# A bucketed attention and a mixture of eight experts in one kernel: where the subtractions of the weights' low halves, the places' matmul, the collection and the remaining capacity stand in the order of work

## The chip, the cores and the metric

The kernel runs on one core of one Trainium2 chip. The metric is device time of one launch in microseconds (us). Engines are named as in the profile: TensorE (PE, its weight loads PEld), VectorE (DVE), ScalarE (ACT), GpSimd (POOL) and SyncE (SP).

## The reference

Attention of 4 x 8 heads over 768 positions of width 64, where a query sees only keys of its own bucket (six signs of a projection), gives x of 3072 tokens by 512. Then a mixture of eight experts, in which the pairs of token and expert are taken in falling order of their score until every expert has its 384 tokens:

```python
cap = N // E                               # 3072 // 8 = 384
logits = x @ w_gate
for idx in np.argsort(-logits.flatten()):
    tok, e = (int(idx) // E, int(idx) % E)
    if assigned[tok] >= 0 or counts[e] >= cap: continue
    assigned[tok] = e
    counts[e] += 1
for e in range(E):
    mask = assigned == e
    h = np.maximum(x[mask] @ w1[e], 0.0)   # 512 x 1024
    out[mask] = h @ w2[e]                  # 1024 x 512
```

## The kernel before

The first 442 us are the attention and the scores; the change leaves them alone. The rest goes expert by expert, in the order in which experts fill up. `run()` (L816 to L852) writes this part out as **slots**, 68 for each expert: 32 slots of `layer1` (three matmuls L775 each) and 36 of `layer2` (two matmuls L787 each). The arithmetic is done in halves: a number is a 16-bit high half and a 16-bit low half, and a product is three matmuls, high by high, low by high and high by low.

**The weights' low halves.** `wload` (L716, GpSimd's indirect DMA) fetches the f32 weights of an expert, `wsplit` cuts them in quarters: ScalarE writes the high half `wh` and scales `wf` (L725, L726), and two subtractions of 128x512 for each quarter make `wl` = `wf` - `wh`. They are put in the list `s.pend`, each with the slot at which it is due. Three places take them from it: `hand(n)` gives n of them to GpSimd (L737), after a small copy `ztick` (L736) that makes GpSimd wait for the step of the moment; `fill()` gives one to VectorE (L741); and a due one is forced on GpSimd by `run()` (L847).

**Choosing the next expert's tokens.** Beside the matmuls of expert k runs phase p = k+1, a generator `phase()` whose parts are put at slots by the tables `EV` (phases 2 to 7; `EV[p]` for p under 5, else `EV[0]`) and `E1` (phase 1). A pair (c0, R) in `EV` gives the first slot, relative to the expert's first, and the distance R of the levels. The parts of a phase, in order:

- the first counting (`count` L504, L505 on TensorE; its last matmul L505 reads `nrem`, the remaining capacity, which ScalarE writes at L567), then the digits (L488) and the comparison L587 on VectorE, at c0;
- the hit (matmul L593, then L597 and a comparison L493 on VectorE), at c0+3;
- four levels of counting (`count4`, at c0+6, c0+6+R, ...) and hit (three slots later), and a last counting at c0+6+4R that ends in `satl` (L604);
- the step that closes the threshold at c0+9+4R (matmuls L607, L608, then on VectorE L611 to L619 with the members' mask `STb`, the weight index `zwidx` L700 and a running sum `cum` L632);
- the **places** (matmuls L635, L636 of `STb` and `cum`), at c0+13+4R, after which VectorE makes the one-hot `ohp` (L644) and `Rr` (L669);
- the **collection** (24 matmuls L646), at c0+22+4R, then the index L688, `close()` (L661 to L667: the new capacity `rem`, the mask `un`), the gather of the tokens (L708) and the next phase's scores and first wide comparison (L475 to L493).

At each part `hand` is called with the number from the list `HS` (phase 1: `H1`). `fill()` is called after the hit of the first counting (L593), after L608, after the places and after the collection. `XD` shifts the slots of the transposes `xsplit` of phases 1 to 3.

Of the kernel before, what the change touches and what calls it, by code (L numbers as in the profile page):

```python
# [14 lines left out]
ALU = mybir.AluOpType  # L15
# [5 lines left out]
 E0=[3, 5],  # L21
 E1=[3, 4],
 X=[2, 2, 5],
# [14 lines left out]
 OPS='b0 i3 i2 t0 b1 w5 r0 r2 w4 s0 w4 C1 r1 t1 c1 s1 B0 c0 D0 w2 w1 s4 w5 s2 s3 r3 v2 w5 v0 l0 l1 C0 m0 s5 w3 s6 r5 w2 l3 e0 e1 d0 u0 u1 s7 v1 l2 w0 m1 e2 | s8 | x0 | w0 | x1 s9 | r4 s10 | | | s11 m2 v3 f0 | x3 | | x2 | m3 | | | | | |')  # L38
PAT,E0,E1,DW,LEAD=(AP[k] for k in ('PAT','E0','E1','DW','LEAD'))
NB=dict(S=2,T=3,V=1)  # L40
# [337 lines left out]
SH=[25,20,15,10,5,0]  # L378
LOW=[1,1,1,1,1,0]
NT=[128,32,32,32,32,32]  # L380
E1=[-12,-4,-3,2,6,8,10,13,16,19,22,25,28,31,34,37,40,48]
H1=[0,0,0,0,0,2,0,2,0,2,0,2,0,2,1,0,0,0]
EV=[(-18,8),(0,0),(-6,7),(-10,7),(-14,7)]
WL=[4,46]
W1=[44,51,58,63]
WS=[0,57,52,48]
HS=[0,1,0,2,0,2,0,3,0,3,1,0,0,0]
BY=[-1,8,40]
W2=[2,7,12,17]
XS=[56,56,57,57]  # L390
XD=[0,7,4,0]
KW=[1,0,4,0,2,19,7,1]
SC=16
XSC=8.0
# [1 line left out]
class Moe:  # L396
# [142 lines left out]
    def phase(s,ph):  # L539

        nc,NC=s.nc,s.NC; V=nc.vector; T=nc.tensor; G_=nc.gpsimd
# [3 lines left out]
        def ps(): return s.ps0() if first and s.ps0 else s.ps()  # L545
# [3 lines left out]
        if not last:  # L549
            P=s.Z  # L550
            D,E,mxu=P["D"],P["E"],P["mxu"]; d=E[:,0]
            CMP=[P["cmp"][l and 1+l%2] for l in range(6)]
            if not first:
                for i,f in enumerate(s.best(P,0,NC)):
                    if ph==1 and i==4: yield
                    f()
                s.gate=P["OH"][0:1,0,0:1]
                for c0,c1_ in ((0,12),(12,NC)) if ph==1 else ((0,NC),):
                    if ph==1: yield
                    s.compare(CMP[0],0,d,c0,c1_)  # L560
                if ph==1: s.gate=CMP[0][0:1,NC//2-1,0,0:1]
            tot=0
            for l,w in enumerate(WID):
                tot+=w; u=2.0**-tot; cmp=CMP[l]
                yield
                pc=ps()
                if l==0 and not first: nc.scalar.mul(s.nrem,s.rem,-1.0/128)  # L567
                if l==0 or first:
                    for c0,c1_ in blocks if first else ((0,NC),):
                        if l: s.compare(cmp,l,d,c0,c1_)  # L570
                        s.count(pc,P,cmp,l,c0,c1_)
                    if first:
                        if l==0: wp=s.wps(); s.warm(KW[7],wp)
                        s.warm(KW[0],wp)
                    for a,b in ((l+1,l+2),) if first else ((1,6),):
                        if a<6:
                            for q in range(a,b): s.digit(P,q,slice(0,NC))
                            if first: V.tensor_tensor(E[:,a:b],D[:,a:b],s.sc[:,a:b],op=ALU.mult)
                            else:
                                for q in range(a,b): nc.scalar.activation(E[:,q],D[:,q],AF.Copy,scale=2.0**-sum(WID[:q+1]))  # L580
                else:
                    nt=s.count4(pc,P,cmp)

                if l==5: break
                sat=t([128,8],BF,"sat"); hit=t([128,1],BF,"hit"); J=NT[l]
                if l==0 or first:
                    V.tensor_scalar(sat[0:J],pc[0:J,0:8],0.0,0.0,op0=ALU.is_ge,op1=ALU.max,accum_out=hit[0:J])  # L587
                else:
                    V.tensor_tensor(sat[0:32],pc[96:128,24:32],nt,op=ALU.is_ge)
                    V.reduce_max(hit[0:32],sat[0:32],axis=AX.X)  # L590
                if not first: yield
                pn=ps(); n=pn[:,0:1]
                T.matmul(n,s.us[l][0:J],hit[0:J],start=True,stop=True)  # L593
                if first: s.warm(KW[1],wp)
                elif l==0: s.fill()
                d2=t([128,NC],BF,"d2",bufs=6); s.gate=d2[0:1,0:1]
                V.scalar_tensor_tensor(d2,d,n,E[:,l+1],op0=ALU.subtract,op1=ALU.add)  # L597
                if not first:
                    s.compare(CMP[l+1],l+1,d2); s.gate=CMP[l+1][0:1,NC//2-1,0,0:1]
                d=d2  # L600

            sat=t([128,8],BF,"satl"); s.gate=sat[0:1,0:1]; nn=t([128,1],F32,"nn"); nf=t([128,1],F32,"nf")
            if first: V.tensor_scalar(sat[0:32],pc[0:32,0:8],0.0,None,op0=ALU.is_ge)
            else: V.tensor_tensor(sat[0:32],pc[96:128,24:32],nt,op=ALU.is_ge)  # L604
            if not first: yield
            pe=ps()
            T.matmul(pe[:,0:8],s.ones,s.wtb,start=True,stop=False)  # L607
            T.matmul(pe[:,0:8],s.tiny[0:32],sat[0:32],start=False,stop=True)  # L608
            if first: s.warm(KW[2],wp)
            else: s.fill()  # L610
            V.reduce_max(nn,pe[:,0:8],axis=AX.X)  # L611
            wg=t([128,NC],F32,"wg"); e0=t([128,NC],F32,"e0"); A1=t([128,8,NC],BF,"A1"); cc=t([128,8],BF,"cc")
            V.tensor_scalar(nf,nn,ROUND*2.0**-32,ROUND*2.0**-32,op0=ALU.add,op1=ALU.subtract)
            V.scalar_tensor_tensor(wg,d,nn,mxu,op0=ALU.is_gt,op1=ALU.mult)
            V.tensor_scalar(cm,nn,nf,2.0**32,op0=ALU.subtract,op1=ALU.mult)
            V.tensor_tensor(s.asg,s.asg,wg,op=ALU.add)
            V.scalar_tensor_tensor(e0,d,nf,mxu,op0=ALU.is_equal,op1=ALU.mult)
            V.tensor_scalar(STb[:,0:NC],s.asg,cm,None,op0=ALU.is_equal)
            V.tensor_scalar(STb[:,NC:],e0,cm,None,op0=ALU.is_equal)  # L619
            s.widx(ph,cm,t)  # L620
        else:
            s8=t([128,8],F32,"s8"); e0=t([128,NC],F32,"e0")
            V.tensor_scalar(c1,s.rem,4.0e4,None,op0=ALU.is_lt)
            V.tensor_tensor(s8,c1,s.wt,op=ALU.mult)
            V.reduce_max(cm,s8,axis=AX.X)
            s.widx(ph,cm,t)
            V.tensor_scalar(e0,s.asg,cm,None,op0=ALU.is_equal)
            V.tensor_tensor(STb[:,0:NC],e0,s.un,op=ALU.add)
            V.memset(STb[:,NC:],0.0)
# [29 lines left out]
        def close(pq):  # L659

            bnd=t([128,8],F32,"bnd")  # L661
            V.tensor_tensor(s.rem,s.rem,pq,op=ALU.subtract)
            V.tensor_scalar(bnd,s.wt,cm,-3.0e38,op0=ALU.is_equal,op1=ALU.mult)
            V.scalar_tensor_tensor(s.rem,bnd,-5.0e4/3.0e38,s.rem,op0=ALU.mult,op1=ALU.add)
            V.tensor_tensor(s.Lm,s.Lm,be(bnd),op=ALU.add)
            V.scalar_tensor_tensor(s.un,wg,0.0,s.un,op0=ALU.is_equal,op1=ALU.mult)
            V.tensor_tensor(s.un,s.un,acc,op=ALU.subtract)  # L667
        def rr():
            for i in range(2): V.tensor_tensor(Rr[:,i],Gt[:,None,i:i+3].to_broadcast([128,2,3,NC]),s.gp[:,i,:,None,:].to_broadcast([128,2,3,NC]),op=ALU.mult)  # L669
        if first:  # L670
            pi=ps()
            for i,b in enumerate(blocks):
                members(*b)
                if not i: rr()
                collect(*b); s.warm(KW[4],wp)
        else:
            members(0,NC)
            rr()
            if not last: left()
            yield  # L680
            pi=ps()
            collect(0,NC)
            if not last:
                T.matmul(pp[:,64:72],s.ones,cc,start=True,stop=True)
                s.fill()
        idx=t([128,3],I32,"idx",bufs=4)
        with nc.allow_low_precision("whole numbers"):
            V.reduce_sum(idx,pi[:,0:12].rearrange("p (z c) -> p c z",z=4),axis=AX.X)  # L688
# [127 lines left out]
    def run(s):  # L816
        V=s.nc.vector; ch=s.ch; at={}; NS=68
# [6 lines left out]
        for p in range(1,8):  # L824
            b=NS*(p-1)
            c0,R=EV[p] if p<5 else EV[0]
            c=[c0,c0+3]
            for l in range(4): c+=[c0+6+R*l,c0+9+R*l]
            c+=[c0+6+4*R,c0+9+4*R,c0+13+4*R,c0+22+4*R]
            ev=[b+e for e in (E1 if p==1 else c)]  # L830
            hs=H1 if p==1 else HS
            dec=ev[-3]
            if p==7: ev=ev[-2:]; hs=[0,0]
            for e,n in zip(ev,hs): add(e,step,p,n)
            add(ev[-1],end,p)
            add(max(dec,b+WL[0]),s.wload,p,0); add(max(ev[-1],b+WL[1]),s.wload,p,1)
            for q in range(4):
                add(b+(WS[p]+4*q if p<4 else W1[q]),s.wsplit,p,0,q,None,b+NS+BY[0]+BY[1]*q if p<6 else 0)
                add(b+XS[q]+(XD[p] if p<4 else 0),s.xsplit,p,q)
        for k in range(8):  # L840
# [64 lines left out]
```

## Time and profile before

| | |
|---|---|
| median of three runs | 771.43 us (770.33 to 774.11) |
| the profiled execution | 773.31 us; its span 771.5 us |
| busy in the span: TensorE, its weight loads | 691.7 us (90%), 441.9 us (57%) |
| VectorE, ScalarE, GpSimd | 546.3 us (71%), 466.6 us (60%), 500.0 us (65%) |
| instructions | 19049 |

All times of single instructions are of the profiled execution, counted from the start of its span. In a timeline an instruction's row ends with the idle time of its engine before it and what ended that; where rows of the same kind follow one another, one row with xcount stands for them. "Granted clock" is the share of TensorE's 2.4 GHz that the chip granted, so 0.5 is 1.2 GHz.

### The profile page before, as it was taken

What the parts mean: (1) busy time and instruction counts of PE and PEld (TensorE: products, weight loads), DVE (VectorE), ACT (ScalarE), POOL (GpSimd) and SP (SyncE); (2) the same over time, 40 slices, a digit from 0 to 9 for tenths busy, and PEclk for the clock granted to TensorE, in tenths of its full rate; (3) what the DMA queues carried; (4) which work ended last, traced back from release to release, by engine and by line L of the source; (5) the groups of instructions that cost most, each with busy time, mean ns of one, the idle gap of its engine ahead of it and who ended that gap; (6) DMA issues with size and microseconds to landing.
All of it is one profiled execution on the core that took longest, in us unless ns stands there. A gap on an engine that the chain in (4) does not pass through costs nothing. (4 is left out here: it accounts for less than half of the span.)

```text
span 771.5 us, 19049 instructions
## 1 busy us (share of the span) xinstructions
PE 691.7 (90%) x7789; PEld 441.9 (57%) x7789; DVE 546.3 (71%) x1170; ACT 466.6 (60%) x858; POOL 500.0 (65%) x445
## 2 busy tenths in 40 slices
PE   8898898999999999988896688888898999999995
PEld 2566665767667667666675544444444555555452
DVE  4979978889888798987756667495868777743120
ACT  6677675677776777755561272817465565656550
POOL 8586859696886969755571546364648384858571
PEclk9999999999999999999997599999999999999998
DMA  7637655428254372500000525334160717162610
GB/s 185 172 102 208 156 148 126 117 73 202 91 127 117 107 196 65 132 29 23 22 22 23 174 86 168 120 120 167 43 258 28 259 42 260 42 221 86 250 45 41
DMA packets 39951, 93.57 MB, mean 121 GB/s; under 512 B 4548, under 2 KB 30520, under 8 KB 37816
## 3 DMA queue, kind: packets, MB, share of 16 engines
q1 hardware_dynamic: 33048, 46.21, 22.8%
q0 software_dynamic: 6816, 46.15, 16.9%
q8 instruction: 61, 1.00, 0.5%
q14 instruction: 26, 0.21, 0.1%
HBM read 59.53 MB, written 12.58 MB: 93 GB/s over the span
## 5 line engine op out<-in xcount | busy, mean ns | idle before, releaser
L255 POOL TENSOR_TENSOR lo<-pt 128x768 f16<-128x768 f32 x143 | 233.4, 1645 | 80.4 <-ACT pt L252 71.0
L252 ACT ACTIVATE pt<-pst 128x384 f32<-128x384 f32 x384 | 182.7, 491 | 95.5 <-PE pst L251 83.5
L228 DVE TENSOR_REDUCE m<-pss 128x1 f16<-128x770 f32 x192 | 182.3, 955 | 41.2 <-PE pss L226 40.1
L250 PE MATMUL pst<-qa,ka 128*128 128x384 f16 x384 | 125.1, 326 | 5.8 <-DVE XT L294 3.1
L251 PE MATMUL pst<-qb,kb 128*128 128x384 f16 x384 | 125.0, 326 | 0.0
L267 PE MATMUL psv<-vh,lo 128*128 128x65 f16 x1152 | 121.1, 194 | 3.3 <-POOL lo L255 3.3
L266 PE MATMUL psv<-vl,pt 128*128 128x64 f16 x1152 | 121.3, 193 | 0.0
L265 PE MATMUL psv<-vh,pt 128*128 128x65 f16 x1152 | 121.2, 195 | 0.0
L265 PEld LDWEIGHTS <-pt 128*128 128x128 bf16 x1152 | 106.7, 98 | 12.7 <-issue 3.1
L266 PEld LDWEIGHTS <-pt 128*128 128x128 bf16 x1152 | 105.8, 99 | 9.6
L226 PE MATMUL pss<-ka,qa 128*128 128x385 f16 x384 | 94.9, 329 | 14.6 <-DVE m L228 13.2
L267 PEld LDWEIGHTS <-lo 128*128 128x128 f16 x1152 | 105.8, 97 | 3.8 <-POOL lo L255 3.7
L725 ACT ACTIVATE wh<-wf 128x1024 f16<-128x1024 f32 x64 | 67.1, 1049 | 33.9 <-PE psa L693 21.1
L737 POOL TENSOR_TENSOR wl<-wf,wh 128x512 f16<-128x512 f32 x71 | 81.2, 1159 | 0.0
L775 PEld LDWEIGHTS <-wh 128*128 128x128 f16 x512 | 48.4, 100 | 33.3 <-issue 5.3
L726 ACT ACTIVATE wf<-wf 128x1024 f32<-128x1024 f32 x62 | 65.5, 1057 | 2.0
L778 DVE SCALAR_TENSOR_TENSOR hl<-px,hh 128x384 f16<-128x384 f32 x64 | 34.7, 552 | 43.7 <-ACT hh L777 43.4
L226 PEld LDWEIGHTS <-qa 128*128 128x128 f16 x384 | 37.4, 98 | 46.2 <-issue 23.7
L787 PEld LDWEIGHTS <-hh 128*128 128x128 f16 x384 | 36.8, 100 | 45.2 <-issue 9.2
L255 DVE TENSOR_TENSOR lo<-pt 128x768 f16<-128x768 f32 x49 | 61.7, 1258 | 1.5 <-ACT pt L252 1.0
L777 ACT ACTIVATE hh<-px 128x384 f16<-128x384 f32 x64 | 30.4, 481 | 49.7 <-PE px L775 49.7
L775 PE MATMUL px<-xl,wh 128*128 128x384 f16 x256 | 57.5, 337 | 0.0
(251 smaller groups left out, 1319.7 us busy)
## 6 DMA issues: line engine op xcount, KB each, us to landing
vp<-in_vv_dram SPq DMA_DIRECT2D x8, 768.0 KB
x_dram<-X SPq DMA_DIRECT2D x16, 384.0 KB
qp<-in_qT_dram SPq DMA_DIRECT2D x7, 768.0 KB
kp<-in_kT_dram SPq DMA_DIRECT2D x7, 768.0 KB
qa<-qh SPq DMA_DIRECT2D x14, 192.0 KB
ka<-kh SPq DMA_DIRECT2D x14, 192.0 KB
qb<-qh SPq DMA_DIRECT2D x14, 192.0 KB
kb<-kh SPq DMA_DIRECT2D x14, 192.0 KB
```

What stands on the lines that cost most here:

```text
L226: T.matmul(ps[:,hf,0:HK],QA[u][:,j,qc*128:qc*128+128],KA[u][:,j,hf*HK:hf*HK+HK],start=True,stop=True)
L228: V.tensor_reduce(M6[h][:,qc:qc+1],ps[:,:,0:HK],axis=AX.XY,op=ALU.max,negate=True)
L250: T.matmul(ps[:,0:384],KA[u][:,j,kr],QA[u][:,j,r],start=True,stop=False)
L251: T.matmul(ps[:,0:384],KB[u][:,j,kr],QB[u][:,j,r],start=False,stop=True)
L252: A.activation(PT[h,kc][0][:,r],ps[:,0:384],AF.Exp,scale=0.125)
L255: eng.tensor_tensor(l,p,p.bitcast(BF)[:,1::2],op=ALU.subtract)
L265: T.matmul(av[:,c,:],ph[:,r],VH[u][:,j,kc,:],start=(kc==0 and c==0),stop=False,skip_group_check=True)
L266: T.matmul(av[:,c,0:64],ph[:,r],VL[u][:,j,kc,:],start=False,stop=False,skip_group_check=True)
L267: T.matmul(av[:,c,:],l[:,r],VH[u][:,j,kc,:],start=False,stop=False,skip_group_check=True)
L725: s.nc.scalar.mul(h[:,r],f[:,r],WSC)
L737: for _ in range(n): s.nc.gpsimd.tensor_tensor(*s.pend.pop(0)[1],op=ALU.subtract)
L775: T.matmul(p[:,0:384],a[:,o:o+128],b[:,d],start=n==0,stop=n==11)
```

## The change

It moves the parts of a phase and the subtractions between them:

- `EV` and `E1`: the first slot is one later for phases 2 and 5 to 7 (p = 2: -6 to -5; p of 5 and more: -18 to -17) and two later for phases 3 and 4; phase 1 keeps its slots up to the places. The places are six slots behind the step before them in place of four (`c0+15+4R`), in phase 1 five in place of three; the collection is eight slots behind the places in place of nine, in phase 1 seven in place of eight.
- `HS` and `H1`: the number of subtractions given to GpSimd at each part; none at the first two parts and none after the last counting, three at three of the levels.
- `fill()`: not any more after L608; a new one after the digits of the first counting, ahead of L587; a second one after the collection.
- `nrem` is written by VectorE at the end of `close()` (L667 of the changed kernel) in place of by ScalarE at the first counting (L567).
- `XD`: the transposes one slot later in phase 1, three in 2, four in 3.

```diff
--- before.py
+++ after.py
@@ -378,17 +378,17 @@
 SH=[25,20,15,10,5,0]
 LOW=[1,1,1,1,1,0]
 NT=[128,32,32,32,32,32]
-E1=[-12,-4,-3,2,6,8,10,13,16,19,22,25,28,31,34,37,40,48]
-H1=[0,0,0,0,0,2,0,2,0,2,0,2,0,2,1,0,0,0]
-EV=[(-18,8),(0,0),(-6,7),(-10,7),(-14,7)]
+E1=[-12,-4,-3,2,6,8,10,13,16,19,22,25,28,31,34,37,42,49]
+H1=[0,0,0,0,0,1,0,2,0,2,0,2,0,2,0,0,0,0]
+EV=[(-17,8),(0,0),(-5,7),(-8,7),(-12,7)]
 WL=[4,46]
 W1=[44,51,58,63]
 WS=[0,57,52,48]
-HS=[0,1,0,2,0,2,0,3,0,3,1,0,0,0]
+HS=[0,0,0,2,0,3,0,3,0,3,0,0,0,0]
 BY=[-1,8,40]
 W2=[2,7,12,17]
 XS=[56,56,57,57]
-XD=[0,7,4,0]
+XD=[0,8,7,4]
 KW=[1,0,4,0,2,19,7,1]
 SC=16
 XSC=8.0
@@ -564,7 +564,6 @@
                 tot+=w; u=2.0**-tot; cmp=CMP[l]
                 yield
                 pc=ps()
-                if l==0 and not first: nc.scalar.mul(s.nrem,s.rem,-1.0/128)
                 if l==0 or first:
                     for c0,c1_ in blocks if first else ((0,NC),):
                         if l: s.compare(cmp,l,d,c0,c1_)
@@ -578,6 +577,7 @@
                             if first: V.tensor_tensor(E[:,a:b],D[:,a:b],s.sc[:,a:b],op=ALU.mult)
                             else:
                                 for q in range(a,b): nc.scalar.activation(E[:,q],D[:,q],AF.Copy,scale=2.0**-sum(WID[:q+1]))
+                                s.fill()
                 else:
                     nt=s.count4(pc,P,cmp)
 
@@ -607,7 +607,6 @@
             T.matmul(pe[:,0:8],s.ones,s.wtb,start=True,stop=False)
             T.matmul(pe[:,0:8],s.tiny[0:32],sat[0:32],start=False,stop=True)
             if first: s.warm(KW[2],wp)
-            else: s.fill()
             V.reduce_max(nn,pe[:,0:8],axis=AX.X)
             wg=t([128,NC],F32,"wg"); e0=t([128,NC],F32,"e0"); A1=t([128,8,NC],BF,"A1"); cc=t([128,8],BF,"cc")
             V.tensor_scalar(nf,nn,ROUND*2.0**-32,ROUND*2.0**-32,op0=ALU.add,op1=ALU.subtract)
@@ -665,6 +664,7 @@
             V.tensor_tensor(s.Lm,s.Lm,be(bnd),op=ALU.add)
             V.scalar_tensor_tensor(s.un,wg,0.0,s.un,op0=ALU.is_equal,op1=ALU.mult)
             V.tensor_tensor(s.un,s.un,acc,op=ALU.subtract)
+            V.tensor_scalar(s.nrem,s.rem,-1.0/128,None,op0=ALU.mult)
         def rr():
             for i in range(2): V.tensor_tensor(Rr[:,i],Gt[:,None,i:i+3].to_broadcast([128,2,3,NC]),s.gp[:,i,:,None,:].to_broadcast([128,2,3,NC]),op=ALU.mult)
         if first:
@@ -682,7 +682,7 @@
             collect(0,NC)
             if not last:
                 T.matmul(pp[:,64:72],s.ones,cc,start=True,stop=True)
-                s.fill()
+                s.fill(); s.fill()
         idx=t([128,3],I32,"idx",bufs=4)
         with nc.allow_low_precision("whole numbers"):
             V.reduce_sum(idx,pi[:,0:12].rearrange("p (z c) -> p c z",z=4),axis=AX.X)
@@ -826,7 +826,7 @@
             c0,R=EV[p] if p<5 else EV[0]
             c=[c0,c0+3]
             for l in range(4): c+=[c0+6+R*l,c0+9+R*l]
-            c+=[c0+6+4*R,c0+9+4*R,c0+13+4*R,c0+22+4*R]
+            c+=[c0+6+4*R,c0+9+4*R,c0+15+4*R,c0+23+4*R]
             ev=[b+e for e in (E1 if p==1 else c)]
             hs=H1 if p==1 else HS
             dec=ev[-3]
```

Lines 568 to 580 and 611 to 667 of before stand one line earlier in the changed kernel; in the rows below its L610 is L611 of before, and so on.

**Place 1**, VectorE in phase 5, from the last counting's `zsatl` (L604) to L614, which makes the weight mask `zwg`; L741 is a subtraction. Before:

```order
L604 TENSOR_TENSOR zsatl<-psa,znt 32x8
L778 SCALAR_TENSOR_TENSOR hl<-px,hh 128x384
L741 TENSOR_TENSOR wl_10473<-wf_10278,wh_10472 128x512
L611 TENSOR_REDUCE znn<-psa 128x1
L613 TENSOR_SCALAR znf<-znn 128x1
L614 SCALAR_TENSOR_TENSOR zwg<-zd_10575,znn,zmxu 128x24
```

and now:

```order
L514 TENSOR_TENSOR znt<-znt,psa 32x8 x2
L604 TENSOR_TENSOR zsatl<-psa,znt 32x8
L610 TENSOR_REDUCE znn<-psa 128x1
L612 TENSOR_SCALAR znf<-znn 128x1
L613 SCALAR_TENSOR_TENSOR zwg<-zd_10575,znn,zmxu 128x24
```

The subtraction L741 and the `hl` between `zsatl` and the threshold's first reduction are gone from there; the `hl` stands ahead.

**Place 2**, GpSimd in phase 2, from the last level's `ztick` to the gather L708; L716 is the load of the next expert's first weights, L847 the forced subtractions. Before:

```order
L736 CAST ztick<-zcmp_381 1x1
L737 TENSOR_TENSOR wl_9408<-wf_9250,wh_9407 128x512 x3
L736 CAST ztick<-zsatl 1x1
L737 TENSOR_TENSOR wl_9408<-wf_9250,wh_9407 128x512
L716 DMA wf_9648<-in_w_dram,zwidx 128x4096
L847 TENSOR_TENSOR wl_9408<-wf_9250,wh_9407 128x512
L708 DMA xg<-x_dram,zidx 128x512 x3
```

and now:

```order
L736 CAST ztick<-zcmp_381 1x1
L737 TENSOR_TENSOR wl_9404<-wf_9251,wh_9403 128x512 x3
L716 DMA wf_9645<-in_w_dram,zwidx 128x4096
L847 TENSOR_TENSOR wl_9404<-wf_9251,wh_9403 128x512 x2
L708 DMA xg<-x_dram,zidx 128x512 x3
```

The copy and the subtraction after `zsatl` are gone, and two forced subtractions stand behind the weight load in place of one. In phase 3 it is two where none stood, in phase 1 one where none stood.

**Place 3**, VectorE in phase 5, from the end of the members' work (L657) to `close()`; L688 reads what the collection gave. Before:

```order
L657 TENSOR_REDUCE zcc<-zA_10637 128x8
L778 SCALAR_TENSOR_TENSOR hl<-px,hh 128x384 x2
L741 TENSOR_TENSOR wl_10473<-wf_10278,wh_10472 128x512
L688 TENSOR_REDUCE zidx<-psa 128x3
L662 TENSOR_TENSOR rem<-rem,psa 128x8
```

and now:

```order
L656 TENSOR_REDUCE zcc<-zA_10630 128x8
L778 SCALAR_TENSOR_TENSOR hl<-px,hh 128x384
L741 TENSOR_TENSOR wl_10452<-wf_10269,wh_10451 128x512 x2
L688 TENSOR_REDUCE zidx<-psa 128x3
L661 TENSOR_TENSOR rem<-rem,psa 128x8
```

There are two subtractions ahead of L688 in place of one, and one `hl` in place of two.

## Rows read from the trace of the kernel before

**Rows 1.** Windows by expert: stretch, us, engines' busy us (instructions), clock, DMA, GB/s
```profile
441.92:489.33 47.41, 40.79 (x302) 22.46 (x301) 30.73 (x113) 25.55 (x44) 20.08 (x25) 0.92 0.43 156
...
731.68:762.98 31.30, 31.30 (x169) 16.32 (x167) 4.27 (x8) 13.22 (x20) 16.63 (x16) 1.00 0.15 60
sum 321.06, PE 295.55 PEld 159.36 DVE 189.93 ACT 181.61 POOL 185.56; mean PE 36.94 PEld 19.92 DVE 23.74 ACT 22.70 POOL 23.19
```

**Rows 2.** TensorE's timeline: start, us, engine, line, operation, [idle before <-releaser]
```profile
469.95 0.20 PE L635 MATMUL psa<-zSTb,ntri 128*128 128x48 bf16 x1 [0.99 <-DVE zwidx L700]
...
512.34 0.20 PE L635 MATMUL psa<-zSTb,ntri 128*128 128x48 bf16 x1 [1.95 <-DVE zwidx L700]
...
555.25 0.22 PE L635 MATMUL psa<-zSTb,ntri 128*128 128x48 bf16 x1 [2.51 <-DVE zwidx L700]
...
595.14 0.20 PE L635 MATMUL psa<-zSTb,ntri 128*128 128x48 bf16 x1 [2.37 <-DVE zwidx L700]
...
634.64 0.20 PE L635 MATMUL psa<-zSTb,ntri 128*128 128x48 bf16 x1 [1.73 <-DVE zwidx L700]
...
673.09 0.20 PE L635 MATMUL psa<-zSTb,ntri 128*128 128x48 bf16 x1 [1.73 <-DVE zwidx L700]
...
714.23 0.53 PE L646 MATMUL psa<-zRr,ohp 128*128 128x12 bf16 x14 [1.67 <-DVE zRr L669]
```

**Rows 3.** Waits: line, what it waited for: total us, times, longest
```profile
PE psa L505 <- ACT nrem L567: 8.5, 5, 2.4
```

**Rows 4.** Windows of the seven stretches among the experts at the lower clock
```profile
674.36:677.77 3.41, 3.41 (x13) 1.60 (x11) 3.34 (x12) 0.48 (x2) 0.88 (x1) 0.50 0.63 130
...
sum 23.88, PE 23.18 PEld 11.08 DVE 15.06 ACT 4.35 POOL 7.90; mean PE 3.31 PEld 1.58 DVE 2.15 ACT 0.62 POOL 1.13
```

**Rows 5.** VectorE's timeline, phase 5, last counting to collection
```profile
630.73 0.97 DVE L741 TENSOR_TENSOR wl<-wf,wh 128x512 f16<-128x512 f32 x1
...
631.88 2.04 DVE L614 SCALAR_TENSOR_TENSOR zwg<-zd,znn,zmxu 128x24 f32<-128x24 bf16 x1
...
636.16 0.25 DVE L651 TENSOR_TENSOR zGt<-zpm,th 128x96 f32<-128x96 f32 x1
...
638.21 0.52 DVE L669 TENSOR_TENSOR zRr<-zGt,gp 128x144 bf16<-128x144 f32 x2
...
640.83 0.16 DVE L688 TENSOR_REDUCE zidx<-psa 128x3 int32<-128x12 f32 x1
```

**Rows 6.** Lines L614, L741: count, ns shortest/median/longest, first and last start
```profile
L614 DVE SCALAR_TENSOR_TENSOR zwg<-zd,znn,zmxu x7: 231/873/2041, 426.8 to 670.3; 128x24 f32<-128x24 bf16 x7
...
L741 DVE TENSOR_TENSOR wl<-wf,wh x20: 680/686/3749, 450.1 to 678.7; 128x512 f16<-128x512 f32 x20
```

**Rows 7.** GpSimd's timeline, phases 2, 5 and 7
```profile
506.75 3.82 POOL L737 TENSOR_TENSOR wl<-wf,wh 128x512 f16<-128x512 f32 x3
...
513.16 1.33 POOL L716 DMA_INDIRECT wf<-in_w_dram,zwidx  x1 [1.37 <-DVE hl L778]
514.51 1.17 POOL L847 TENSOR_TENSOR wl<-wf,wh 128x512 f16<-128x512 f32 x1
...
632.73 1.14 POOL L737 TENSOR_TENSOR wl<-wf,wh 128x512 f16<-128x512 f32 x1
...
709.40 2.26 POOL L847 TENSOR_TENSOR wl<-wf,wh 128x512 f16<-128x512 f32 x2
```

**Rows 8.** VectorE's timeline, phases 1, 2 and 7
```profile
449.13 0.56 DVE L778 SCALAR_TENSOR_TENSOR hl<-px,hh 128x384 f16<-128x384 f32 x1 [2.76 <-ACT hh L777]
...
513.87 1.94 DVE L651 TENSOR_TENSOR zGt<-zpm,th 128x96 f32<-128x96 f32 x1
...
709.37 2.33 DVE L650 TENSOR_SCALAR zmi<-zpm 128x24 int32<-128x24 int32 x1
```

**Rows 9.** Timelines of VectorE, then TensorE, at the first counting of phase 6
```profile
644.00 1.75 DVE L493 TENSOR_TENSOR zcmp<-zE,tb 128x3072 bf16<-128x3072 bf16 x1
...
645.82 0.75 PE L504 MATMUL psa<-zOH,zcmp 128*128 128x8 bf16 x24
```

## The prediction

> **What bounds the kernel now.** I read the windows by expert first, then the waits, then the timelines of TensorE, VectorE and GpSimd where the waits fall. The attention part (to 441.9 us) is left as it is by the change; I look at the eight experts only. Expert 7, which has no choosing beside it, shows what TensorE needs: 31.30 us, busy all of it, for 68 slots [rows 1], so a slot is about 0.46 us. The eight experts together take 321 us [rows 1]; 8 x 31.3 is 250. Of the 71 us between, the choosing's own matmuls take a part; the rest is TensorE waiting for the choosing of the next expert. The waits name two places: the places' matmul L635, six waits of 0.99, 1.95, 2.51, 2.37, 1.73 and 1.73 us, 11.28 in all [rows 2], and L505, which waits for ScalarE's capacity `nrem`, 8.5 us in five waits [rows 3]. The first is longest just where VectorE is between the last counting and the places. After such waits the granted clock falls to its lower level, 1.2 GHz, for 3.41 us: seven stretches, 23.88 us [rows 4]. At half clock such a stretch costs about 1.7 us. Four follow L635, two L505, one L646.
>
> **What ends L635's wait.** Phase 5 is the clear case: a subtraction L741 on VectorE takes 0.97, then L614 takes 2.04 [rows 5] where the shortest of its kind takes 0.23 [rows 6]. It ends at 633.92, when GpSimd's subtraction after `zsatl` ends, at 632.73 + 1.14 = 633.87 [rows 7]. So VectorE is held while GpSimd subtracts. L635 starts 0.72 after L614 ends.
>
> **The change part by part.**
>
> *L635, two slots more, no L741 ahead of L614, no GpSimd subtraction after `zsatl`.* Phase 5: L614 would start 0.97 earlier than 631.88 and take 0.23, so L635 could start at 631.14 + 0.72 = 631.86. TensorE arrived at 634.64 - 1.73 = 632.91, and will arrive 0.92 later. The wait is gone with 2 us to spare; so for phases 1 and 6. In phases 2 to 4 GpSimd's batch of three after the last level still stands: 3.82 us from 506.75, to 510.57 [rows 7]; L614 ends no earlier, so L635 could start at 510.6 + 0.72 = 511.3, against TensorE's arrival at 512.34 - 1.95 + 0.92 = 511.31. All move on together by the phase's own later start, and GpSimd has a third subtraction more at an earlier level, so I leave 0.5 us each. Gain 11.28 - 1.5 = **9.8**. The four low-clock stretches behind it: 4 x 1.7 = **6.8**.
>
> *Capacity on VectorE.* `nrem` becomes one small instruction after the capacities are closed (some 0.15 us), long before L505. Phase 1 keeps almost nothing of its 2.4: there VectorE stands in order behind an `hl` that waits 2.76 us for ScalarE and ends at 449.7 [rows 8]; the hit that TensorE needs next is as late as before, so 0.2. The others give 8.5 - 2.4 = 6.1. What replaces them: the first-counting subtraction now waits for ScalarE's first weight quarter, and xh stands behind one weight quarter more on ScalarE; I charge 1.1. Gain **5.2**. Two low-clock stretches go: **3.4**.
>
> *Collection, one slot fewer after the places (8 instead of 9; 7 instead of 8 in phase 1).* From L635 to the second L669 VectorE takes 634.64 to 638.73 = 4.1 us in phase 5 [rows 2, 5]; 8 slots and the places' pair give TensorE about 4.1. So it just fits where nothing holds VectorE. But in phases 1, 2 and 3 GpSimd now issues the weight load L716 and right behind it one, two and two forced subtractions (L847), as nothing is left at the places to take them on VectorE before slot 40. The trace has this once, in phase 2, with one: L716 513.16, L847 514.51 to 515.68 [rows 7]; VectorE's L651, 0.25 when free [rows 5], took 1.94 [rows 8], a loss of 1.7. Two lose 1.7 + 1.17 = 2.85: phase 7's L650 took 2.33, through the end of two L847 [rows 7, 8]. So waits at L646 of 2.8 in phases 2 and 3, each with a low-clock stretch (2 x 4.5 = 9.0), 1.0 in phase 1, where VectorE may come ahead of the one, and a third of a stretch (1.5 in all), 0.8 in phase 4 (late by its batch), 0.25 in 5 and 6 each. Phase 7's own wait of 1.67 [rows 2] halves, since its places come three slots later behind a GpSimd that does not move, and half a stretch goes: -1.7. Cost **10.1**. Bounds: nothing, if VectorE slips in ahead of L847; 3.6 each, if the L741 ahead is caught too.
>
> The Trainium skill (SBUF — State Buffer, Who interferes with whom) has a rule that speaks for a smaller loss: the port pair of VectorE and GpSimd is an exclusive lock held for one whole instruction, and the one that issued first gets it. By it VectorE would get in between two L847, and the loss would be 1.7 in phases 2 and 3 also: 7 us less in all with phase 1's and the stretches. The trace agrees in part: something got in between at one batch, of 3.82 where 3 x 1.14 is 3.4 [rows 7], but L650 waited out two [rows 8].
>
> *First counting of phases 5 and 6: two subtractions at the collection, and two or one slots fewer (12 and 13 for 14).* In the trace L688 comes 2.1 after the second L669's end with one L741 between; two make it 2.8 (0.69 each [rows 6]). L688 to the end of the wide compare: 645.75 - 640.83 = 4.9 [rows 5, 9]. With `nrem` the compare ends 2.8 + 4.9 + 0.15 = 7.85 after L669. TensorE, released by L669, now takes 7.1 to L504 at 645.82 [rows 9], 0.7 of it for the collection and 14 slots of 0.46; with 12 or 13 it will be there after 6.2 or 6.65. So L504 waits 1.65 and 1.2, and some of a stretch follows (1.3). Cost **4.2**. Bounds: 0 and 6.3, both stretches in full.
>
> *Batches of three at one more level.* L614's kin at each level is held by them at times; 0 to 3 us, I take **1.5**.
>
> *At no cost*: moves of the transposes (the gathered tokens land with the same distance), the extra subtraction before L587 in phases 2 to 6 otherwise (covered by TensorE's L504 and three slots).
>
> **Sum.** -9.8 - 6.8 - 5.2 - 3.4 + 10.1 + 4.2 + 1.5 = -9.4. The profiled execution took 773.31 (span 771.5), 1.9 above the median 771.43; 771.4 - 9.4 = **762.0**.
>
> **Rivals.**
> *A: VectorE slips in between GpSimd's subtractions.* Collection in phases 2 and 3 waits 1.7 instead of 2.8, half of their stretches go, phase 1 waits not at all, the batches cost nothing: 762.0 - 2.2 - 1.7 - 1.5 - 1.5 = **755**. For it: the batch of three that lasts 3.82 [rows 7]. Against: L650 [rows 8]. By the skill's rule above it is this case. Chance 0.17.
> *B: ScalarE's wait only changes its place.* The new L741 in front of L587 waits for ScalarE as L505 did, the hit comes as late, and the 5.2 and 3.4 are not had: **770.6**. Against: it needs the first quarter, where `nrem` stood behind two in phases 2 to 4. Chance 0.15.
> *C: slower.* GpSimd becomes the bound: three batches of three in a row at the levels, and if every L597 behind one waits out the whole batch as L614 did (2.04 - 0.23 = 1.8, less some 0.3 of slack), ten levels in five phases cost 10 x 1.5 = 15 in place of 1.5: **775.5 to 777**, say 776. It decides from the point where a batch outlasts the seven or eight slots of a level (3.2 to 3.7 against 3.5 to 3.8). Against: two such batches stand in a row now, and no count among the waits is long. Chance 0.10.
>
> **How the numbers follow.** Forecast 0.58, A 0.17, B 0.15, C 0.10. The forecast's own range is 756 to 769, from the bounds above taken half way. For 8 in 10: **752 to 772**, which leaves out C and the outer ends of the others. A difference under 0.5% (3.9 us) can't be told from none. Faster by more (below 767.6): nine tenths of the forecast, and A, **0.69**; within: the rest of it, and B, **0.21**; slower: C, **0.10**.
>
> **What would show it.** L635: waits of at most 0.6, L614 at 0.23 in phases 1, 5, 6. No `nrem` among TensorE's waits. L646: 2 to 3.5 us in phases 2 and 3, with L651 or its neighbour held until the second L847 ends. L504: 1 to 2 us in phases 5 and 6. Low-clock stretches among the experts: about five in place of seven, at other places. It is wrong if the collection waits of phases 2 and 3 are below 1 us, if the hit's matmul L593 waits over 1 us in phases 2 to 4, or if L635 still waits over 1 us.

## The result, and the profile after

The changed kernel takes **762.44 us** (median of four runs, 760.39 to 763.70) against 771.19 us (770.33 to 774.11): a ratio of 0.9877, 95% interval 0.9842 to 0.9913. Forecast were 762.0 us and 752 to 772. The total came out almost exactly; several of its terms did not, and their errors went in opposite directions.

The profiled execution of the changed kernel took 763.70 us (span 761.9). The windows by expert of the changed kernel, columns as in [rows 1]:

```profile
444.26:489.63 45.37, 39.02 (x296) 21.27 (x295) 31.79 (x116) 24.69 (x40) 18.69 (x21) 0.92 0.43 150
...
722.08:753.38 31.30, 31.30 (x169) 16.32 (x167) 4.18 (x8) 13.32 (x20) 16.75 (x16) 1.00 0.17 68
sum 309.12, PE 288.62 PEld 155.78 DVE 193.35 ACT 180.32 POOL 178.19; mean PE 36.08 PEld 19.47 DVE 24.17 ACT 22.54 POOL 22.27
```

The eight experts take 309.12 us where they took 321.06 [rows 1], 11.9 less; expert 7 is at 31.30 as before. The attention part, which the change leaves alone, took 2.3 us more in this execution (444.26 for 441.92), with two low-clock stretches that the profiled execution of before did not have. In the profiled executions of all kernels below, that part (up to the first L775) ends between 440.5 and 444.8 us, though no edit touches it. A difference of a few us between two medians is thus not always the experts'; where it matters, the time of the experts in the profiled executions is given beside it.

TensorE's timeline of the changed kernel, its waits from the hit of phase 1 to phase 7's collection (columns as in [rows 2]):

```profile
454.16 0.16 PE L593 MATMUL psa<-zhit,us 128*128 128x1 bf16 x1 [3.91 <-DVE zsat L587]
...
475.40 0.38 PE L787 MATMUL po<-wl,hh 128*128 128x512 f16 x1 [0.78 <-POOL wl L847]
...
489.63 0.48 PE L775 MATMUL px<-xh,wh 128*128 128x384 f16 x2 [0.69 <-DVE xl L751]
...
515.97 0.38 PE L787 MATMUL po<-wl,hh 128*128 128x512 f16 x1 [0.64 <-POOL wl L847]
517.08 0.38 PE L787 MATMUL po<-wl,hh 128*128 128x512 f16 x1 [0.73 <-POOL wl L847]
...
519.52 0.56 PE L645 MATMUL psa<-zRr,ohp 128*128 128x12 bf16 x15 [1.21 <-DVE zRr L669]
...
532.69 0.48 PE L775 MATMUL px<-xh,wh 128*128 128x384 f16 x2 [0.72 <-DVE xl L751]
...
558.47 0.71 PE L645 MATMUL psa<-zRr,ohp 128*128 128x12 bf16 x21 [2.75 <-DVE zRr L669]
...
592.38 0.20 PE L634 MATMUL psa<-zSTb,ntri 128*128 128x48 bf16 x1 [0.27 <-DVE zwidx L700]
...
596.99 0.47 PE L645 MATMUL psa<-zRr,ohp 128*128 128x12 bf16 x12 [0.63 <-DVE zRr L669]
...
604.24 0.76 PE L504 MATMUL psa<-zOH,zcmp 128*128 128x8 bf16 x24 [0.98 <-DVE zcmp L493]
...
640.99 0.76 PE L504 MATMUL psa<-zOH,zcmp 128*128 128x8 bf16 x24 [0.79 <-DVE zcmp L493]
...
705.50 0.66 PE L645 MATMUL psa<-zRr,ohp 128*128 128x12 bf16 x19 [1.45 <-DVE zRr L669]
```

The places (L634 here) wait 0.27 us once, where they waited six times and 11.28 us [rows 2]; L505 waits for no capacity [rows 3]. In their place stand a hit of phase 1 that waits 3.91, layer 2 itself waiting for `wl` (2.15 us in three waits, the forecast has nothing of it), the collection, and `xl` at the start of an expert. All of TensorE's waits over 0.2 us among the experts add up to 24.2 us before and 19.7 after: **the waits give only 4.5 of the 11.9 us.** Most of the rest is the clock:

```profile
451.08:457.91 6.83, 3.75 (x19) 1.89 (x19) 4.21 (x18) 4.40 (x10) 1.30 (x2) 0.50 0.02 7
560.31:563.72 3.41, 3.41 (x10) 1.20 (x9) 3.35 (x13) 2.36 (x4) 2.55 (x3) 0.50 0.51 135
707.08:710.50 3.42, 3.42 (x10) 1.22 (x9) 0.00 (x0) 0.00 (x0) 2.54 (x3) 0.50 0.99 417
sum 13.66, PE 10.58 PEld 4.31 DVE 7.56 ACT 6.76 POOL 6.40; mean PE 3.53 PEld 1.44 DVE 2.52 ACT 2.25 POOL 2.13
```

These are the windows of the changed kernel at the granted clock 0.50 among the experts: 13.66 us, four stretches of 3.41 (two run together after the hit of phase 1). Before there were eight, not the seven of [rows 4]: one at L505 of phase 1 was left out there, a window of the kernel before:

```profile
449.08:452.49 3.41, 3.24 (x13) 1.56 (x13) 2.45 (x11) 2.77 (x10) 0.07 (x1) 0.50 0.02 7
```

Four fewer, at some 1.7 us each (an estimate: half of 3.41), are 6.8. 4.5 + 6.8 = 11.3, and 11.9 is what is seen. The estimate is too high for the changed kernel's first stretch in phase 1: it begins at 451.08, within the hit's wait (450.25 to 454.16), and TensorE is busy for only 3.75 of the two stretches' 6.83 us, so the two together cost about 1.9 and not 3.4.

### The profile page after: what moved, and what is told of

It reads as the page before. It is cut to its first block, busy times and chain, and to the rows that moved or that the text cites. A ratio compares the mean times of both kernels' runs of the same rounds, so it can differ in the third digit from the quotient of the medians.

```text
span 761.9 us, 19025 instructions
## 1 busy us (share of the span) xinstructions
PE 687.1 (90%) x7789; PEld 440.1 (58%) x7789; DVE 550.4 (72%) x1180; ACT 465.7 (61%) x852; POOL 493.2 (65%) x431
## 5 line engine op out<-in xcount | busy, mean ns | idle before, releaser
L265 PEld LDWEIGHTS <-pt 128*128 128x128 bf16 x1152 | 107.3, 98 | 12.9 <-issue 3.5
L737 POOL TENSOR_TENSOR wl<-wf,wh 128x512 f16<-128x512 f32 x64 | 72.1, 1146 | 0.0
L775 PEld LDWEIGHTS <-wh 128*128 128x128 f16 x512 | 48.3, 98 | 37.2 <-issue 8.3
L790 ACT ACTIVATE o<-po 128x512 f32<-128x512 f32 x24 | 14.3, 594 | 70.4 <-PE po L787 70.3
L775 PE MATMUL px<-xh,wh 128*128 128x384 f16 x256 | 55.5, 329 | 1.7 <-DVE xl L751 1.4
```

The source lines that it names most:

```text
L265: T.matmul(av[:,c,:],ph[:,r],VH[u][:,j,kc,:],start=(kc==0 and c==0),stop=False,skip_group_check=True)
L737: for _ in range(n): s.nc.gpsimd.tensor_tensor(*s.pend.pop(0)[1],op=ALU.subtract)
L775: T.matmul(p[:,0:384],a[:,o:o+128],b[:,d],start=n==0,stop=n==11)
```

## The experiments

All ratios are against the kernel before on the same chip (its medians 770.6 to 771.4), with 95% intervals. Three parts are told apart: the **capacity** (`nrem` on VectorE), the **slots** (`EV`, `E1`, `XD`, places and collection) and the **subtractions** (`fill()`, `HS`, `H1`); together they are the change.

**The capacity alone.**

```diff
-                if l==0 and not first: nc.scalar.mul(s.nrem,s.rem,-1.0/128)
...
+            V.tensor_scalar(s.nrem,s.rem,-1.0/128,None,op0=ALU.mult)
```

> The kernel before with only the capacity's move (VectorE writes nrem at the end of close). Theory, the forecast's own term: L505 waits for nothing in phases 2 to 4 and 6 (6.1 us), phase 1's wait only moves to the hit L593, two low-clock stretches go (3.4): 8 to 9 us, so about 762.5; all of L635's waits stay (11.3 us in six). Rival: TensorE then waits as long for what follows (hit L593 or xl), because ScalarE is the late one: under 3 us gained, 768 or more.

766.18 us, 0.9921 (0.9887 to 0.9955): 5.1 us. Between the two theories. Its five executions lie in two groups, 761.8 and 762.8, and 766.2 to 767.0; the profiled one is of the lower group. L505 waits no more, phase 1's hit waits 1.20, and a hit of phase 2, which waited 0.95, waits 2.50. The places' waits stay, 11.1 us in six.

**All but the capacity.**

```diff
+                if l==0 and not first: nc.scalar.mul(s.nrem,s.rem,-1.0/128)
...
-            V.tensor_scalar(s.nrem,s.rem,-1.0/128,None,op0=ALU.mult)
```

> The changed kernel with the capacity back on ScalarE at the first counting. Theory (parts add): the 8.6 us of the capacity's term are lost, about 771, with waits of 1.4 to 2.4 us at L505 in phases 1 to 4 and a low-clock stretch behind two of them. Rival: the new subtraction ahead of L587 waits for ScalarE all the same, so that the capacity costs little beside it: 764 or less.

775.21 us, 1.0036 (1.0013 to 1.0059): slower than before. The parts do not add: the slots and the subtractions cost 3.9 us without the capacity and bring some 3.7 with it, and the capacity, worth 5.1 alone, is worth 12.8 in the changed kernel. TensorE's timeline of this kernel, L505:

```profile
528.54 0.17 PE L505 MATMUL psa<-nrem,moneh 128*128 128x8 f16 x1 [2.54 <-ACT nrem L567]
...
572.29 0.17 PE L505 MATMUL psa<-nrem,moneh 128*128 128x8 f16 x1 [2.23 <-ACT nrem L567]
...
613.43 0.17 PE L505 MATMUL psa<-nrem,moneh 128*128 128x8 f16 x1 [1.48 <-ACT nrem L567]
```

With phases 1, 2 and 6 it is 11.2 us, against 8.5 [rows 3]. The places no longer wait, so TensorE comes to L505 sooner; ScalarE, which cuts weights in order ahead of `nrem`, does not. The wait that one part removes is collected by the next.

**The slots, with the capacity.**

```diff
-EV=[(-18,8),(0,0),(-6,7),(-10,7),(-14,7)]
+EV=[(-17,8),(0,0),(-5,7),(-8,7),(-12,7)]
...
-            c+=[c0+6+4*R,c0+9+4*R,c0+13+4*R,c0+22+4*R]
+            c+=[c0+6+4*R,c0+9+4*R,c0+15+4*R,c0+23+4*R]
```

(and `E1`, `XD` as in the change)

> Before with the capacity on VectorE and the new slots (EV, E1, XD, places six slots on, collection eight), but the subtractions where they were (L741 ahead of L614, one on GpSimd after zsatl). Theory (both the slots and the subtractions held the places): places come 0.92 later, so L635 waits 0.1, 0.7, 1.6, 1.5, 0.8, 0.8 us in phases 1 to 6, L645 about 1 us in phases 2 and 3; some 763.5 against 766.2 with the capacity alone. Rival (the slots do it alone): no L635 wait over 0.5 us, 762.5 or less. Rival 2 (the collection one slot nearer gives it all back): 766 or more.

765.22 us, 0.9920 (0.9896 to 0.9945): 1 us from the capacity alone, which can't be told from nothing. The places wait 6.0 us in place of 11.1, much as the theory had it wait by wait, but the collection, the hit of phase 1 (3.19) and `xh` and `xl` take it back.

**The subtractions, with the capacity.** `fill()`, `HS` and `H1` as in the change, `EV`, `E1`, `XD` and the places of before.

> Before with the capacity on VectorE and the subtractions moved (none ahead of L614, none on GpSimd after zsatl, one ahead of L587, two after the collection, the new lists), but the slots of before. Theory: L635 waits for nothing in phases 1, 5 and 6, about 1 us in phases 2 to 4, where GpSimd's last batch of three still holds L614; L504 waits for nothing in phases 5 and 6 (14 slots); forced subtractions hold the collection of phase 2; the hit of phase 1 waits over 3 us. About 763. Rival (the moved subtractions do it alone): no L635 wait over 0.4, 761 or less. Rival 2 (they only hinder, the slots are the gain): 766 or more.

758.91 us, 0.9846 (0.9815 to 0.9878), under the rival's 761 though two of its places' waits are left. **The subtractions are the gain; that the new slots add anything to it is not seen.** The median is 3.5 us under the changed kernel's, but the intervals overlap (0.9842 to 0.9913 there), and in the profiled executions the experts take 307.21 us against 309.12: the rest of the difference lies in the attention part. TensorE's timeline of this kernel, the only waits at the places over 0.2 us:

```profile
508.87 0.20 PE L634 MATMUL psa<-zSTb,ntri 128*128 128x48 bf16 x1 [0.28 <-DVE zwidx L700]
...
549.66 0.20 PE L634 MATMUL psa<-zSTb,ntri 128*128 128x48 bf16 x1 [1.14 <-DVE zwidx L700]
```

At the places 1.4 us are left for the slots to remove. Elsewhere they do remove something: here a hit of phase 2 waits 2.78 us (at 493.47), in the changed kernel 0.75; its waits for `wl` and `xl` stand against that, and all waits over 0.2 us add up to 18.5 us here and 19.7 there.

**One subtraction of GpSimd's, or one of VectorE's.** With the capacity on VectorE, first only GpSimd's subtraction after `zsatl` is moved to an earlier level:

```diff
-HS=[0,1,0,2,0,2,0,3,0,3,1,0,0,0]
+HS=[0,1,0,2,0,3,0,3,0,3,0,0,0,0]
```

(`H1` likewise)

> The kernel before with the capacity on VectorE and only GpSimd's subtraction after zsatl moved, to an earlier level (phase 1 too); VectorE's own L741 stays ahead of L614. Theory (GpSimd holds VectorE, the forecast's reading of rows 5 to 7): L614 lasts under 0.5 us in phases 5 and 6 and L635 waits there 0.1 to 0.3 us in place of 1.74; in phases 2 to 4 the batch of three before it holds on, 1 to 2 us. About 762.5 against 766.2. Rival (VectorE's own subtraction is what is in the way): L635 still waits over 1 us in phases 5 and 6, 765 or more.

then only VectorE's L741 from ahead of L614 to ahead of L587:

```diff
-            else: s.fill()
             V.reduce_max(nn,pe[:,0:8],axis=AX.X)
...
                                 for q in range(a,b): nc.scalar.activation(E[:,q],D[:,q],AF.Copy,scale=2.0**-sum(WID[:q+1]))
+                                s.fill()
```

> The kernel before with the capacity on VectorE and only VectorE's subtraction moved from ahead of L614 to ahead of L587; GpSimd's after zsatl stays in phases 2 to 7. Theory: L614 waits out GpSimd's subtraction all the same, so L635's waits in phases 5 and 6 stay within 0.3 us of 1.74; the hit of phase 1 waits about 3.5 us. About 766. Rival: L635 waits under 1 us in phases 5 and 6, 763 or less.

759.33 us, 0.9852 (0.9828 to 0.9877), and 761.44 us, 0.9883 (0.9862 to 0.9904). The waits of the places (us; a dash is under 0.2):

| phase | 1 | 2 | 3 | 4 | 5 | 6 |
|---|---|---|---|---|---|---|
| capacity alone | 1.05 | 1.61 | 2.53 | 2.40 | 1.74 | 1.74 |
| and the slots | - | 0.82 | 1.84 | 1.80 | 0.77 | 0.78 |
| and GpSimd's subtraction moved | - | 0.94 | 2.07 | 0.77 | 0.46 | 0.48 |
| and VectorE's moved | - | 1.35 | 1.59 | 1.91 | 0.93 | 0.94 |
| and all subtractions moved | - | 0.28 | 1.14 | - | - | - |
| the change | - | - | - | 0.27 | - | - |

Neither theory is whole: in phase 5 moving GpSimd's subtraction takes 1.28 of the 1.74 away, moving VectorE's own takes 0.81, and with all subtractions moved none of it is left. In time the first can't be told from all subtractions moved (759.33 and 758.91 us; the experts 306.71 and 307.21), so with the capacity on VectorE, giving one subtraction of GpSimd's in each phase at another level has all of the change's gain that can be seen. VectorE's timeline, phase 5, with the capacity alone (L613 is L614 of before):

```profile
623.85 0.98 DVE L741 TENSOR_TENSOR wl<-wf,wh 128x512 f16<-128x512 f32 x1
...
625.01 2.04 DVE L613 SCALAR_TENSOR_TENSOR zwg<-zd,znn,zmxu 128x24 f32<-128x24 bf16 x1
```

with GpSimd's subtraction moved:

```profile
621.65 1.51 DVE L741 TENSOR_TENSOR wl<-wf,wh 128x512 f16<-128x512 f32 x1
...
623.35 0.23 DVE L613 SCALAR_TENSOR_TENSOR zwg<-zd,znn,zmxu 128x24 f32<-128x24 bf16 x1
```

and with VectorE's moved:

```profile
621.88 0.23 DVE L613 SCALAR_TENSOR_TENSOR zwg<-zd,znn,zmxu 128x24 f32<-128x24 bf16 x1
...
622.41 1.95 DVE L617 TENSOR_SCALAR zSTb<-asg,zcm 128x24 bf16<-128x24 f32 x1
```

The loss is not L614's own: whichever instruction meets GpSimd's subtraction carries it. In the last kernel L613 is through in time, and L617 lasts until 624.36, when GpSimd's subtraction has ended. GpSimd's timeline there:

```profile
622.02 1.01 POOL L796 DMA_INDIRECT out_dram<-o,zidx  x1 [0.16 <-DVE znf L612]
...
623.17 1.14 POOL L737 TENSOR_TENSOR wl<-wf,wh 128x512 f16<-128x512 f32 x1
```

The hold begins at 622.41, before the subtraction does, while GpSimd still issues the scatter L796; so does that of L614 in the kernel before (631.88, the subtraction from 632.73 [rows 5, 7]). The scatter alone does not hold VectorE: with GpSimd's subtraction moved, L613 (623.35, 0.23, above) passes within one.

```profile
622.78 1.27 POOL L796 DMA_INDIRECT out_dram<-o,zidx  x1 [0.16 <-issue]
```

**None forced behind the weight load.** The changed kernel with more subtractions given to GpSimd at the levels of phases 1 to 3:

```diff
-H1=[0,0,0,0,0,1,0,2,0,2,0,2,0,2,0,0,0,0]
+H1=[0,0,0,0,0,2,0,2,0,2,0,2,0,2,0,0,0,0]; HS3=[0,1,0,3,0,3,0,3,0,3,0,0,0,0]
...
-            hs=H1 if p==1 else HS
+            hs=H1 if p==1 else HS3 if p<4 else HS
```

> The changed kernel with two subtractions more given to GpSimd at the levels of phases 2 and 3 and one more in phase 1, so that none is forced behind the weight load. Theory (forced subtractions behind L716 cost what the collection loses): the waits for wl at L787 (0.78, 0.64, 0.73 us) go, L645 waits under 0.7 us in phases 2 and 3 in place of 1.21 and 2.75, the stretch at 560 us goes: 5 to 7 us less than the changed kernel, about 756.5. Rival (GpSimd's longer batches hold the hits): the hits of phases 1 to 3 wait 1 us and more at several levels, and the time is 761 or more. Rival 2 (the collection is short of slots, not of GpSimd): L645 still waits 2 us in phase 3, about 760.

760.76 us, 0.9843 (0.9814 to 0.9871). All waits that the theory names are gone as it says (none for `wl`, L645 0.69 in phase 3 and under 0.2 in phase 2, no stretch there), and yet only some 1.7 us of 5 to 7 are had (2.1 in the experts' part of the profiled executions, 306.98 for 309.12), too little to be told from none by the times. Timelines of TensorE, VectorE and ScalarE at the first level of phase 3:

```profile
529.70 0.32 PE L511 MATMUL psa<-zOH,zcmp 128*128 128x32 bf16 x6 [2.32 <-DVE zcmp L493]
```

```profile
528.74 0.25 DVE L597 SCALAR_TENSOR_TENSOR zd<-zE,psa 128x24 bf16<-128x24 bf16 x1 [3.23 <-ACT zE L579]
```

```profile
526.46 1.04 ACT L725 ACTIVATE wh<-wf 128x1024 f16<-128x1024 f32 x1
527.53 1.06 ACT L726 ACTIVATE wf<-wf 128x1024 f32<-128x1024 f32 x1
528.50 0.66 ACT L579 ACTIVATE zE<-zD 128x24 bf16<-128x24 int32 x5
```

VectorE's L597, right ahead of the comparison L493, now waits 3.23 us for the digits `zE`, which ScalarE writes at 528.50 behind the weights it cuts in order. It is neither rival: TensorE arrives sooner, and ScalarE is the next that is late.

**The first weights cut later.** The changed kernel, with ScalarE's cutting of expert 0's second weights at slots 8, 11, 14, 17:

```diff
-add(NS*k+W2[q],s.wsplit,k,1,q,None,NS*k+BY[2] if k<6 else 0)
+add(NS*k+(W2[q] if k else 8+3*q),s.wsplit,k,1,q,None,NS*k+BY[2] if k<6 else 0)
```

> The changed kernel with ScalarE's cutting of expert 0's second weights started at slot 8 in place of 2 (then 11, 14, 17). Theory (phase 1's wait is ScalarE held in order behind a weight transfer that lands late, not the added subtraction): the hit L593 of phase 1 waits under 0.7 us in place of 3.91, and the two low-clock stretches at 451 us go: 3 + 3.4, so about 756. Rival (the subtraction ahead of L587 makes the wait): L593 still waits over 2 us, 761 or more.

757.06 us, 0.9805 (0.9783 to 0.9826): 5.4 us less than the changed kernel. What held the changed kernel in phase 1 shows on ScalarE:

```profile
449.91 1.06 ACT L725 ACTIVATE wh<-wf 128x1024 f16<-128x1024 f32 x1 [1.47 <-DMA wf<-in_w_dram,zwidx]
450.99 1.06 ACT L726 ACTIVATE wf<-wf 128x1024 f32<-128x1024 f32 x1
451.96 0.47 ACT L777 ACTIVATE hh<-px 128x384 f16<-128x384 f32 x1
```

and on VectorE, both of the changed kernel:

```profile
452.46 0.56 DVE L778 SCALAR_TENSOR_TENSOR hl<-px,hh 128x384 f16<-128x384 f32 x1 [3.75 <-ACT hh L777]
...
453.33 0.69 DVE L741 TENSOR_TENSOR wl<-wf,wh 128x512 f16<-128x512 f32 x1
453.94 0.16 DVE L587 TENSOR_SCALAR_CACHE_REDUCE zsat<-psa 128x8 bf16<-128x8 f32 x1
```

ScalarE stands in order at a weight transfer that lands at 449.9; `hh` behind it, `hl` behind that on VectorE, and the digits and L587 behind `hl`. The subtraction ahead of L587 is 0.6 of the 3.91 us. How late the transfer is differs from run to run: ScalarE idles 1.47 us for it here, 0.63 in the kernel before, and not at all with the capacity alone, where the hit waits 1.20. ScalarE's row of before, then that of the capacity alone:

```profile
446.58 1.06 ACT L725 ACTIVATE wh<-wf 128x1024 f16<-128x1024 f32 x1 [0.63 <-DMA wf<-in_w_dram,zwidx]
...
446.07 1.04 ACT L725 ACTIVATE wh<-wf 128x1024 f16<-128x1024 f32 x1
```

So ScalarE idles 0.84 us longer at the transfer than before; whether the change has a part in that was not tried. With the cutting later the hit waits

```profile
448.71 0.16 PE L593 MATMUL psa<-zhit,us 128*128 128x1 bf16 x1 [0.30 <-DVE zsat L587]
```

and the two stretches of phase 1 are gone. The hit's 3.6 us and the stretches' 1.9 add up to the 5.4 us seen.

**Both of these together, and with earlier transposes.** The two edits in one kernel, then also `XD=[0,8,6,3]`.

> The changed kernel with the first weights of expert 0 cut later and no forced subtraction behind the weight load (the two edits that took 5.4 and 1.7 us alone). Theory (parts add): 755.4, L593 of phase 1 under 0.7 us, no wait for wl, L645 under 0.7. Rival (VectorE and ScalarE are late at the levels instead, as in the waits of 1.1 to 2.3 us at L775 and L511 that the second edit brought): 757 or more.

> The same as the kernel with the late first weights and none forced, and the transposes of phases 2 and 3 one slot earlier (XD 0, 8, 6, 3). Theory (xl at the first slot of layer 1 is late because the transposes stand too late): the waits of 0.70 and 0.73 us at L775 and those for xh go, 1 to 2 us less. Rival (ScalarE and VectorE are busy there and xl comes when it comes): no change within 0.5 us, or a wait at the transposes for the gathered tokens.

755.23 us, 0.9794 (0.9772 to 0.9815), and 755.59 us, 0.9805 (0.9784 to 0.9825). The first is as the theory of adding parts has it, though its rival's waits at the levels (2.33 and 1.96 us at L511) are there too. The earlier transposes change nothing that can be told: the wait of 0.70 at L775 stays at the start of expert 1 and goes at that of expert 2, and phase 3's first level waits 2.26.

**The subtractions with the slots of before, and the first weights later; then phase 2 without forced ones** (`HS2=[0,0,0,3,0,3,0,3,0,4,0,0,0,0]` for it).

> The kernel of the moved subtractions with the slots of before and the capacity on VectorE (758.9 us), and the first weights of expert 0 cut later (an edit that took 5.4 us from the changed kernel). Theory (parts add): 753.5, L593 of phase 1 under 0.7 us. Rival (the old slots bring the same wait elsewhere in phase 1): 757 or more.

> The same, and in phase 2 two subtractions more at the levels (3, 3, 3, 4), so that none is forced behind the weight load. Theory: L645 of phase 2 waits under 0.8 us in place of 2.07 and wl is in time (0.35), but L634 waits up to 1 us for the batch of four: 1 to 2 us less than without. Rival (the batches hold the hits and the places as much): no gain or a loss of 1 us.

754.60 us, 0.9793 (0.9767 to 0.9818), and 755.89 us, 0.9832 (0.9776 to 0.9889). The first beats the changed kernel by 7.8 us and takes none of its slots; it can't be told from the 755.23 above. In the second L645 of phase 2 and `wl` do come in time and L634 waits 1.23 as feared. The times show no gain, but one of its four executions took 762.91; in the profiled executions the experts take 301.05 us against 302.82, about what its theory has, on one profile of each. It stays unclear.

## Why the prediction was right in its sum, and where its steps failed

By the traces of the two kernels (a low-clock stretch at 1.7 us):

| term | forecast | in the traces |
|---|---|---|
| L635 and its four stretches | -9.8 - 6.8 | -11.0 - 6.8 |
| capacity: L505, what replaces it, stretches | -5.2 - 3.4 | -8.45 + 3.91 + 1.41 - 1.7 = -4.8 |
| collection | +10.1 | +2.15 + 4.37 + 1.7 = +8.2 |
| first counting of phases 5 and 6 | +4.2 | +1.8 |
| batches of three | +1.5 | +1.2 |

The capacity's sum is L505's 8.45 less the hit of phase 1 (3.91), `xl` (0.69 + 0.72) and one stretch, as three stood at L505 before and two stand at that hit now. The collection's is `wl` (0.78 + 0.64 + 0.73), L645 (1.21 + 2.75 + 0.63 + 1.45 less the 1.67 of before) and the stretch at 560.31. The batches are waits of hits, levels and `wl` in phases 2 to 4, 3.2 us for 2.0. Together the traces have -11.4 of the 11.9; with the hit's two stretches at 1.9 in all it would be -12.9, so these sums hold to about 1 us.

**L635.** The size is right and so is L614 as the place; "two slots more" is not what did it. The term took three causes together. The table of waits shows that, with the capacity on VectorE, the moved subtractions alone leave 1.4 us of 11.1, while the slots alone leave 6.0. So the forecast's first term belongs for the most part to the subtractions, and the slots added nothing to the time that can be seen. Nor did L614 fall to 0.23 in phase 5, as the forecast's signs had it: it takes 0.67 there in the changed kernel, and 1.71 and 2.27 in phases 3 and 4, held by the batch of three, but VectorE is early enough there all the same.

**Capacity.** "Phase 1 keeps almost nothing of its 2.4" (0.2) was too kind: there TensorE waits 3.91 in place of 2.36, and two stretches stand there in place of one. The step saw `hl` behind ScalarE [rows 8] and did not follow ScalarE further back, to the transfer it stands at; of the 1.55 us more, 0.6 is the added subtraction, and ScalarE idled 0.84 longer for the transfer than in the profile of before. This is rival B, which took all phases, confined to one phase. Elsewhere the wait is gone and stays gone.

**Collection.** The forced subtractions did hold VectorE through two of them, as forecast: L650 of the changed kernel in phase 2 took 3.04 us,

```profile
514.11 3.04 DVE L650 TENSOR_TENSOR zGt<-zpm,th 128x96 f32<-128x96 f32 x1
```

to 517.15, with GpSimd's two from 514.75 to 517.03. Rival A, in which VectorE slips in between, falls at these places. But a step was left out: what GpSimd writes there is needed by layer 2 itself three slots after it is due. TensorE waits for `wl` first (0.64 and 0.73 in phase 2), and that shortens the wait at L645 behind it to 1.21 of the 2.8 forecast. In phase 3, where the collection comes before that slot, it is 2.75 and a stretch, as forecast. That this cost could be had back by giving GpSimd the work earlier, as one would conclude from the term, was not seen: that run brought 1.7 us.

**First counting.** 0.98 and 0.79 us in place of 1.65 and 1.2, and no stretch: the stretch was charged in part and did not come. **Rival C** falls: no hit behind a batch waits over 0.75 us.

So the forecast was right in the main because the places' waits go with their stretches, as it said. That it came within 0.4 us of the measured time is luck twice over: too little was charged in phase 1 and for `xl` and too much at the collection and the first counting; and in the profiled executions the experts gained 11.9 us where the sum had 9.4, while the attention part took 2.3 more.

## What to carry to other kernels

A wait that goes brings TensorE sooner to the next engine that is late, so the worth of one edit depends on the others: the capacity was worth 5 us alone and 13 in the changed kernel, and the other edits without it made the kernel slower (by 3.9 us). Before a term is credited to several edits at once, ask which of them the row's numbers need: here moving two subtractions removed most of the wait, and the new slots added no gain that can be seen. When a wait ends at an engine that works in order, follow that engine back until something is late by itself; in phase 1 this was a weight transfer, and cutting its weights later was worth 5.4 us, as much as the capacity alone. And look at what no edit touches: here the attention part of the profiled executions differed by up to 4.3 us, as much as several of the steps that were compared.

## What the runs showed of the hardware that was not expected

**A long wait is not always followed by a low-clock stretch.** With the capacity alone, the places of phase 3 waited 2.53 us and those of phase 4 2.40. Windows of that kernel, the stretch behind each:

```profile
551.67:555.08 3.41, 3.32 (x11) 1.31 (x10) 3.38 (x10) 0.49 (x1) 1.34 (x1) 0.50 0.47 86
...
589.90:593.30 3.40, 3.31 (x21) 1.89 (x22) 3.37 (x9) 0.98 (x2) 1.33 (x1) 1.00 0.39 72
```

In the same time TensorE does 11 instructions at 0.50 and 21 at 1.00. Before, phase 4's wait of 2.37 was followed by one. Waits of 1.73 were followed by a stretch in phase 6 of before and by none in phase 5. So a stretch is a chance that comes with a wait, at 1.7 us, and one profile counts them with luck; executions of one kernel lie 5.2 us apart with the capacity alone (five) and 6.7 with all but the capacity (ten).

**How long GpSimd holds VectorE.** The hold fell on whichever instruction came (L614, L617, L649, L650, L741). It could begin before the subtraction, while GpSimd issued a transfer ahead of it (L617 and L614 above; L650 in the 3.04 above, from 514.11, the first subtraction from 514.75), and why it begins there is not shown. It ended with GpSimd's run of subtractions at most places, two of them in 3.04 above, and in one case three: with the capacity alone, phase 3, an L741 from 546.60 lasted 3.77 while GpSimd subtracted from 545.20 to 548.58 and again from 548.67 to 549.81. In phase 2 of the changed kernel, though, L613 (510.74, 0.23) came through within a batch of three (508.67 to 512.04), and the next held one, L615, 1.06. The rule of the Trainium skill (SBUF — State Buffer, Who interferes with whom), that the pair of ports is held for one instruction by whoever issued first, agrees with the latter and does not explain the former. What decides between them was not tried.
